# Folding a linear attention into its output projection, in hand-set order, and a new opening for the token mixer

## The chip, the cores and the metric

The kernel runs on one core of one Trainium2 chip. The metric is the device time of one execution in microseconds (us). Times are medians over several executions; the profile and trace of one execution give the rest. The span in a profile is 1.7 to 2.2 us shorter than the measured time of that execution. Some executions list a granted clock of 0.996 or 0.997 in place of 0.999 or 1.0.

## The reference

A block with two halves: a linear attention with 32 heads of 32, and a two-layer MLP over the tokens (the "token mixer"). S = 2048 tokens, D = 1024, F = 3584, bf16 inputs. The code is shortened.

```python
def _A_ref(x, wqkv, wo):
    qkv = (x @ wqkv).reshape(B, S, 3, H, Dh).transpose(2, 0, 3, 1, 4)
    q, k, v = qkv[0], qkv[1], qkv[2]
    phi = lambda t: jnp.where(t > 0, t + 1, jnp.exp(t)) + 1e-6
    pq, pk = phi(q), phi(k)
    kv = jnp.einsum("bhsd,bhse->bhde", pk, v)
    z = jnp.einsum("bhsd->bhd", pk)
    num = jnp.einsum("bhqd,bhde->bhqe", pq, kv)
    den = jnp.einsum("bhqd,bhd->bhq", pq, z)[..., None] + 1e-6
    return (num / den).transpose(0, 2, 1, 3).reshape(B, S, D) @ wo

def _B_ref(x, w1, b1, w2, b2):
    h = _layernorm(x, axis=-1)
    u = _gelu(jnp.einsum("bsd,sf->bdf", h, w1) + b1)
    return (jnp.einsum("bdf,fs->bds", u, w2) + b2).transpose(0, 2, 1)

h  = x + _A_ref(_layernorm(x), A_wqkv, A_wo)
h2 = h + _B_ref(_layernorm(h), B_w1, B_b1, B_w2, B_b2)
```

## The kernel before

The core has five engines. TensorE (PE) multiplies into PSUM; VectorE (DVE) and ScalarE (ACT) read PSUM and prepare operands; SyncE (SP) issues nearly all DMAs. A scheduler may move instructions within an engine's stream, unless the kernel holds them in program order with `pin`. Four stages follow one another: the projections with the sum of kv over the tokens; the attention (query projections, numerator and denominator, output projection, normalization of h); mixer 1 (h with w1); mixer 2.

In the attention each of the 16 tiles of 128 tokens gets its own numerators and denominators, its division on VectorE, and a transpose by DMA back into `pqT`; then the output projection.

```python
def attn_num_den(i):
    for j in range(ND):                       # 8 matmuls of 132 columns
        b, sl = divmod(j, JPB)
        nc.tensor.matmul(nd_ps[:, b, sl * NCOL:(sl + 1) * NCOL],
                         lhsT=pqT[:, j, i * P:(i + 1) * P], rhs=ndrhs[:, j, :], start=True, stop=True)
    # ... Ln and Exp of the denominators on ScalarE, o_sb = num * rd on VectorE
    return o_sb

def attn_transpose(i, o_sb):
    nc.sync.dma_start_transpose(out=pqT[:, :, i * P:(i + 1) * P], in_=o_sb[:])

def out_proj(i):
    xr = xrs.pop(i)
    h_bf = a3w.tile([P, D], BF16, name="h_bf")            # pool a3w: 3 buffers
    for dc in range(NDC):                                 # 2 halves of 512 columns
        ap_ = acc_tile()
        nc.scalar.copy(ap_[:, 0:CW], xr[:, dc * CW:(dc + 1) * CW])   # the residual as a seed
        # ... 8 matmuls of pqT with wo_sb added to it (cuts are marked with ...)
        nc.scalar.copy(h_bf[:, dc * CW:(dc + 1) * CW], ap_[:, 0:CW])
        nc.vector.bn_stats(st[:, dc, :], ap_[:, 0:CW])
    # ... bn_aggr, Ln, Exp
    nc.sync.dma_start(h_dram[i][:], h_bf[:])

def normalize_h(i):
    dst = hE if i % 2 == 0 else hO                        # even tiles, odd tiles
    nc.vector.tensor_scalar(dst[:, i // 2, :], h_bfs.pop(i)[:], ...)
    if i % 2 == 1:
        combine(hE[:, q, :], hO[:, q, :], hT2[:, q, :], hT3[:, q, :], hT4[:, q, :])   # 4 VectorE ops
```

The mixer uses the seven products of the Strassen-Winograd scheme, M1 to M7, for each pair of output tiles. From the second group of pairs on, M1 and M5 are themselves split into seven half-sized "inner" products, whose matmuls (`psI`, 256 columns) alternate with those of an outer product, in the hope that PE has outer work while VectorE and ScalarE add up the inner ones:

```python
def interleave(self, n, fs):
    # ... steps of the outer products fs, cut into four parts
    for f in (n.i1, 0, n.i6, n.i2, 1, n.i5, n.i7, 2, n.i3, 3, n.i4):
        fill(f) if isinstance(f, int) else f()

def run_pair(st, pend, nxt, ...):             # the first two pairs of mixer 1, one after the other
    st.p1()
    # ...
    if not pend:
        h = st.nk // 2
        st.p5(list(range(st.nk - 1))); st.p2(list(range(h))); st.p5([st.nk - 1])
    # ... p6, rest of p2, p7, p3, with the weight sums for the next pair between them
```

## Time and profile before

| | before |
|---|---|
| time, median of 3 | 573.17 us (573.12 to 573.37) |
| span of the profiled execution | 571.5 us |
| PE busy | 563.7 us, 99% |
| last kv accumulation to first mixer matmul ("attention") | 109.64 us |
| mixer 1 | 167.53 us |
| mixer 2 | 165.03 us |
| PE waits in mixer 1, by matmul start times | 3.1 us |

The stage lengths and PE waits here and below are worked out from the start times of the matmuls in the trace: a wait is what the distance between two starts has above columns / 2400 + 0.0025 us, which is the pace at which the matmuls of this kernel follow one another (0.216 us for 512 columns, 0.109 us for 256).

The first lines of the profile page of before: busy time by engine, and the chain of waits, that is, the chain of work that ended last, as shares of the span.

```profile
span 571.5 us, 8308 instructions
...
PE 563.7 (99%) x3124; PEld 293.3 (51%) x3124; DVE 390.2 (68%) x759; ACT 272.0 (48%) x585; POOL 1.8 (0%) x8
...
PE 95%; DVE 3%; ACT 1%; issue 1%; DMA 1%; ACTq 0%
```

PE is the bound almost everywhere. VectorE at 68% is not on the chain. A gain must come from less PE work or from the few PE waits.

The timeline of PE in the attention of before (start, duration, engine, line, operation, output <- input, count; in after, L208 is the line of a helper through which all held instructions go, so there the tile names tell them apart; SPq is SyncE's queue):

```profile
134.55 0.63 PE L1118 MATMUL nd_ps<-ndrhs,pqT 128*128 128x132 bf16 x8
135.02 3.61 PE L1019 MATMUL acc_t<-xnT,wq_sb 128*128 128x512 bf16 x16
```

Each tile's numerator and denominator take 0.47 us (from 134.55 to 135.02), 7.5 us for the 16 tiles. The printed durations have PE's latency in them; starts are what to subtract.

The timeline of PE where mixer 1 opens, in before; in brackets, the idle time before a group and what ended it:

```profile
235.50 1.68 PE L297 MATMUL psA<-hE,wq 128*128 128x512 f16 x7
237.34 0.38 PE L297 MATMUL psA<-hE,wq 128*128 128x512 f16 x1 [0.15 <-DVE hE L1189]
...
239.96 1.02 PE L297 MATMUL psA<-hO,wq 128*128 128x512 f16 x4 [0.74 <-ACT psB L316]
```

M1 (psA) runs out of normalized tiles, and M2 waits for the ScalarE copy that frees psA. With two smaller waits these are 1.46 us by start times.

### The profile page before, as it was taken

What the parts mean: (1) busy time and instruction counts of PE and PEld (TensorE: products, weight loads), DVE (VectorE), ACT (ScalarE), POOL (GpSimd) and SP (SyncE); (2) the same over time, 40 slices, a digit from 0 to 9 for tenths busy, and PEclk for the clock granted to TensorE, in tenths of its full rate; (3) what the DMA queues carried; (4) which work ended last, traced back from release to release, by engine and by line L of the source; (5) the groups of instructions that cost most, each with busy time, mean ns of one, the idle gap of its engine ahead of it and who ended that gap; (6) DMA issues with size and microseconds to landing.
All of it is one profiled execution on the core that took longest, in us unless ns stands there. A gap on an engine that the chain in (4) does not pass through costs nothing.

```text
span 571.5 us, 8308 instructions
## 1 busy us (share of the span) xinstructions
PE 563.7 (99%) x3124; PEld 293.3 (51%) x3124; DVE 390.2 (68%) x759; ACT 272.0 (48%) x585; POOL 1.8 (0%) x8
## 2 busy tenths in 40 slices
PE   7999999999999999999999999999999999999997
PEld 3444444455554444346555565555445655645643
DVE  6898887546767879873735627453979749659625
ACT  4747777666667776445445354453220411311211
POOL 1000000000000000000000000000000000000000
PEclk9999999999999999999999999999999999999999
DMA  9933432029536753104041340413892932912111
GB/s 303 357 76 79 89 74 38 19 96 323 118 72 127 177 178 111 55 2 147 1 148 28 120 148 1 148 48 81 205 255 84 244 96 75 278 56 73 38 47 46
DMA packets 97800, 66.61 MB, mean 117 GB/s; under 512 B 32082, under 2 KB 91744, under 8 KB 97760
## 3 DMA queue, kind: packets, MB, share of 16 engines
q1 hardware_dynamic: 97024, 65.42, 41.7%
q10 hardware_dynamic: 672, 0.66, 0.3%
q8 instruction: 24, 0.39, 0.3%
q14 instruction: 16, 0.13, 0.1%
q0 software_dynamic: 64, 0.01, 0.0%
HBM read 50.34 MB, written 8.39 MB: 103 GB/s over the span
## 4 chain that ended last, share of the span: by engine, by line
PE 95%; DVE 3%; ACT 1%; issue 1%; DMA 1%; ACTq 0%
PE psB L297 10%; PE psC L297 10%; PE acc_t L1019 9%; PE acc_t L1167 9%; PE psC L208 7%; PE psA L297 7%; PE psI L230 7%; PE psB L208 6%; PE psI L208 6%; PE psB L750 4%; PE psC L750 4%; PE psA L750 4%; PE psA L208 3%; PE acc_t L674 2%; PE psE L750 2%; PE psE L297 1%
## 5 line engine op out<-in xcount | busy, mean ns | idle before, releaser
L297 PEld LDWEIGHTS <-sa 128*128 128x128 f16 x436 | 42.6, 98 | 46.8 <-issue 0.7
L1019 PE MATMUL acc_t<-xnT,wq_sb 128*128 128x512 bf16 x256 | 58.0, 379 | 0.0
L1167 PE MATMUL acc_t<-wo_sb,pqT 128*128 128x512 bf16 x256 | 56.1, 379 | 0.0
L208 PEld LDWEIGHTS <-wq 128*128 128x128 bf16 (+1 forms) x357 | 34.5, 98 | 31.3
L297 PEld LDWEIGHTS <-wq 128*128 128x128 bf16 (+1 forms) x324 | 31.6, 98 | 33.1 <-issue 1.0
L208 PE MATMUL psC<-gs,wq 128*128 128x512 f16 (+2 forms) x210 | 45.0, 365 | 0.0
L1167 PEld LDWEIGHTS <-pqT 128*128 128x128 bf16 x256 | 24.8, 98 | 29.0
L1019 PEld LDWEIGHTS <-wq_sb 128*128 128x128 bf16 x256 | 24.5, 98 | 27.4
L166 ACT ACTIVATE e_sb<-acc_t 128x512 bf16<-128x512 f32 x40 | 23.9, 597 | 26.5 <-PE acc_t L1019 24.3
L170 DVE TENSOR_SCALAR e_sb<-e_sb 128x512 bf16<-128x512 bf16 x64 | 18.5, 289 | 25.4 <-ACT e_sb L166 24.8
L208 PEld LDWEIGHTS <-sa 128*128 128x128 f16 x231 | 22.6, 98 | 18.6
L750 PEld LDWEIGHTS <-xs 128*128 128x128 f16 x208 | 20.0, 98 | 23.3 <-DVE xs L736 1.3
L208 DVE TENSOR_TENSOR ot<-ot,hr 128x512 bf16<-128x512 bf16 (+2 forms) x27 | 11.2, 415 | 28.1 <-ACT ot L406 27.7
L333 ACT COPY psC<-psB 128x512 f32<-128x512 f32 x22 | 12.5, 570 | 35.1 <-PE psB L297 21.5
L297 PE MATMUL psB<-hT,sa 128*128 128x512 f16 x112 | 28.4, 379 | 0.0
L441 DVE TENSOR_TENSOR e<-psI,es 128x256 f32<-128x256 f32 x12 | 5.1, 425 | 34.0 <-PE psI L230 34.0
L297 PE MATMUL psC<-hT,wq 128*128 128x512 f16 x112 | 28.3, 379 | 0.0
L750 PE MATMUL psA<-wkv,xnT 128*128 128x512 bf16 x104 | 26.7, 379 | 0.0
L1178 DVE BATCH_NORM_STATS2 hst<-acc_t 128x6 f32<-128x512 f32 x32 | 22.1, 692 | 6.7 <-ACT h_bf L1177 6.5
L297 PE MATMUL psA<-hO,wq 128*128 128x512 f16 x112 | 25.6, 379 | 0.7 <-ACT psB L316 0.7
L297 PE MATMUL psB<-hO,sa 128*128 128x512 f16 x112 | 25.5, 379 | 0.0
L297 PE MATMUL psC<-hT,sa 128*128 128x512 f16 x112 | 25.5, 379 | 0.0
(184 smaller groups left out, 1022.9 us busy)
## 6 DMA issues: line engine op xcount, KB each, us to landing
wq<-in_B_w_dram SPq DMA_DIRECT2D x14, 1024.0 KB, 7.7
wq<-in_B_w_dram SPq DMA_DIRECT2D x8, 1792.0 KB, 9.1
xr<-in_A_x_dram SPq DMA_DIRECT2D x16, 256.0 KB, 3.1
h_dram<-h_bf SPq DMA_DIRECT2D x16, 256.0 KB, 2.2
hr<-h_dram SPq DMA_DIRECT2D x32, 128.0 KB, 2.4
out_dram<-ot SPq DMA_DIRECT2D x31, 128.0 KB, 1.8
x_sb<-in_A_x_dram SPq DMA_DIRECT2D x15, 256.0 KB, 3.2
wkv<-in_A_wqkv_dram SPq DMA_DIRECT2D x2, 1024.0 KB, 9.0
```

The lines of the kernel that those rows point to most:

```text
L166: pin(nc.scalar.activation(e_sb[:], src, ACT.Exp))
L170: pin(nc.vector.tensor_scalar(e_sb[:], e_sb[:], 1.0, PHI_EPS, ALU.min, ALU.add))
L208: return (lambda *a, **kw: pin(op(*a, **kw))) if Held.on else op
L230: pe.matmul(ps, lhsT=self.lhs[m][:, k, :], rhs=self.mov[m][:, k, :], start=(start and k == 0), stop=(k == self.nk - 1), skip_group_check=True,
L297: pe.matmul(ps[:, cols], lhsT=lhs[:, k, :], rhs=mv(k)[:, cols], start=(start and k == 0), stop=(k == self.nk - 1), skip_group_check=True,)
L333: nc.scalar.copy(self.C[:], self.B[:])
L441: dve.tensor_tensor(self.sts[m].e[:, self.cols(h)], ps, es, ALU.add)
L674: mm = nc.tensor.matmul(pp[:, 0:CW], lhsT=xnT[:, kt, i * P:(i + 1) * P], rhs=wkv[:, kt, c * CW:(c + 1) * CW], start=(kt == 0), stop=(kt == ...
L750: pin(nc.tensor.matmul(ps[:], lhsT=lhs[:, k, :], rhs=rhs[:, k, :], start=(start and k == 0), stop=(k == hk2 - 1), skip_group_check=True,))
L1019: nc.tensor.matmul(qp[:, 0:SW], lhsT=wq_sb[:, kt, j * P:(j + 1) * P], rhs=xnT[:, kt, u * SW:(u + 1) * SW], start=(kt == 0), stop=(kt == ND ...
L1167: nc.tensor.matmul(ap_[:, 0:CW], lhsT=pqT[:, j, i * P:(i + 1) * P], rhs=wo_sb[:, j, dc * CW:(dc + 1) * CW], start=(j == 0 and not SEED_RES ...
L1178: nc.vector.bn_stats(st[:, dc, :], ap_[:, 0:CW])
```

## The change

Three parts. **Folding:** kv is folded into wo once (8 transposes, 16 matmuls of 512 columns); denominators are made for 512 tokens at once, with four 32-column matmuls side by side on PE's columns; their reciprocals are written to DRAM and broadcast back over the partitions; VectorE scales `pqT` with them, and the output projection uses the folded weights. Nearly everything in this part is held in program order, on all engines. **Mixer 1's opening:** M1 and M2 of both first pairs come first, and the first M5 is an inner product. **Evacuations:** large evacuations of interleaved outer products are issued behind the inner copies. The diff, cut to its core:

```diff
+    hv, ht, hs, hd = (Held(e, True) for e in (nc.vector, nc.tensor, nc.scalar, nc.sync))   # always pinned
 ...
-            def attn_num_den(i): ...          # and attn_transpose, the o_sb and nd_ps tiles
+            def fold(j):
+                for c in range(NDC):
+                    cols = slice(c * CW, (c + 1) * CW)
+                    ps = acc_tile()
+                    ht.matmul(ps[:, 0:CW], lhsT=kvT[:, j, :], rhs=wo_sb[:, j, cols], start=True, stop=True)
+                    (hs.copy if c == 0 else hv.tensor_copy)(wf[:, j, cols], ps[:, 0:CW])
+
+            def den_mm(u):
+                ps = ndp.tile([P, SW], F32, tag="den", name="den_ps")
+                for o in range(2):
+                    for g in range(4):
+                        j = 4 * o + g
+                        ht.matmul(ps[g * QR:(g + 1) * QR, :],
+                            lhsT=zz[:, j, (1 - o) * HB:(1 - o) * HB + QR],
+                            rhs=pqT[:, j, u * SW:(u + 1) * SW],
+                            start=(o == 0), stop=(o == 1), ..., tile_position=(0, g * QR))
+                return ps
+
+            def den_inv(u, ps):
+                rd = a3d.tile([P, SW], FP16, tag="rd", name="rd")
+                hs.activation(ps[:], ps[:], ACT.Ln, bias=eps_den[:], scale=1.0 / S)
+                hs.activation(rd[:], ps[:], ACT.Exp, scale=-1.0)
+                hd.dma_start(rd_dram[u][:], rd[:])
+                rows = rd_dram[u].rearrange("(g o h) n -> o h g n", g=4, h=HB)
+                for h in range(2):
+                    rdb = a3d.tile([P, NH, SW], FP16, tag="rdb", bufs=3, name="rdb")
+                    for q in range(HB):
+                        hd.dma_start(rdb[q * DH:(q + 1) * DH, :, :],
+                            rows[h, q].unsqueeze(0).to_broadcast([DH, 4, SW]))
+                    rdbs[u, h] = rdb
+
+            def scale_q(u, h):
+                v = pqT[:, h * NH:(h + 1) * NH, u * SW:(u + 1) * SW]
+                hv.tensor_tensor(v, v, rdbs.pop((u, h))[:], ALU.mult)
 ...
+            scale_at = {0: (NSC - 2, 1), 4: (NSC - 1, 0), 5: (NSC - 1, 1)}
             for i in range(NS):
-                if i % 2 == 0 and i // 2 < TPC:
-                    attn(NS - TPC + i // 2)
 ...
-                out_proj(i)
-                if i >= 2:
-                    normalize_h(i - 2)
+                seed(i + 1)
+                out_mm(i)
+                if i == 0:
+                    den(NSC - 1)
+                load_xr(i + XRL + 2)
+                if i > 0:
+                    h_scale(i - 1)
+                if i == NS - 1:
+                    normalize_h(i - 2)
+                    normalize_h(i - 1)
+                out_evac(i)                        # h_bf copies, statistics, store of h
+                if i in scale_at:
+                    scale_q(*scale_at[i])
+                if 2 <= i < NS - 1:
+                    normalize_h(i - 2)
 ...                                            # and the first weight sums, spread over the tiles
-            for f in (n.i1, 0, n.i6, n.i2, 1, n.i5, n.i7, 2, n.i3, 3, n.i4):
+            for f in (n.i1, after1, 0, n.i6, n.i2, 1, n.i5, n.i7, flush, 2, n.i3, 3, n.i4, flush):
 ...
-    pend = run_pair(cur, [], nxt)
 ...
-    pend = run_pair(cur, pend, nxt, after1=sums1, after5=sums5)
+    Held.on = True
+    sums5()
+    cur.mov5 = mov5
+    pend, nxt = cur.run_first(quad1(1), sums1)     # p1 p1 p2 p2, inner M5 with both p6, p7 p7 p3 p3
```

## The prediction

> **What bounds the kernel now.** TensorE. The page gives PE 99% of the 571.5 us span, and the chain of waits is PE for 95%. The chain also shows the pace: 16 matmuls of 512 columns in 3.45 us (0.216 us each), 8 of 256 in 0.87 us (0.109 us), and every num/den block of 8 x 132 columns adds 0.47 us between q units. Summing these costs over all 3124 matmuls gives 558 us; by matmul start times only about 9 us of the span is PE waiting, more than half of it in the first 20 us, which the change leaves alone. Only less PE work, or the few waits after 130 us, can pay. The timeline shows those: 1.5 us where the mixer opens (PE waits at 237.3 for the normalized hE tile, at 240.0 for the copy psA to psB, 0.74 us), 0.8 us at 261-270, and about 0.2 us in each of five later inner/outer interleaves: near 3.3 us in all.
>
> **What the change does to PE work** (estimates from those durations):
> - removes 128 num/den matmuls: -7.4 us;
> - adds 8 kv transposes (+0.5) and 16 fold matmuls of 512 columns, kv into wo (+3.5);
> - adds 32 denominator matmuls of 512 columns in four 32-column positions. The Trainium skill, "TensorE: Matmul & The Clock Gate", Part 3, says matmuls in different column groups run concurrently (2.38x for three); "TensorEngine Tiling (Array Packing)", Key Properties, says a mode switch drains the array. No run of this kernel shows either. Concurrent: 8 x 0.216 us plus eight drains, I estimate 3 us in all; serial: 6.9 us;
> - first M5 of mixer 1 as 28 half matmuls (3.05 us) for 16 full ones (3.45): -0.4 us.
> Sum: about -0.8 us; +3 us if the column groups do not overlap.
>
> **Off the critical path.** DVE loses o_sb (23 us) and the memset, gains eight 128x2048 scalings (about 1.2 us each by similar tiles), 8 fold evacuations and earlier mixer sums. ACT loses the small Ln/Exp (8.5 us), gains eight 128x512 ones (0.6 each), a kvT copy and 8 fold copies (0.58): in the fold stretch about 1.8 us per 2.16 us of PE. DMA loses 16 transposes and gains four round trips: write (about 2.2 us), then eight 128 KB broadcasts, against a scaling placed some 10-11 us later. That is tight, as a late broadcast stops DVE and then PE; five accumulators absorb a few us.
>
> **Waits removed.** M1 and M2 of both pairs give 7 us of work while the last tile is normalized, so the 1.5 us at the opening should nearly vanish. Large evacuations behind the inner copies should remove most of the 0.2 us per interleave and part of the 0.8: together -2.5 us. New small waits at transposes, mode switches and the first scaling: +0.3 to +1 us.
>
> **Prediction.** -0.8 - 2.5 + 0.5: 570.3 us rounded in the change's favour to 570.0; range 566.5 to 573.5. Faster by over 2%: 2%; within 2%: 96%; slower by over 2%: 2%.
>
> **What would show each step.** Matmul start times in the denominator groups: about 0.22-0.3 us per group of four if concurrent, 0.86 if serial. The timeline between last output projection and inner M5: no PE wait above 0.2 us. Interleaves: psI waits under 0.05 us. PE waits after 130 us near 1 us in sum. DVE scaling not waiting for DMA over 2 us. Mixer 2 unchanged.
>
> **What would make it wrong.** Serial column groups (+3.9 us); the scaling late, starving the q units; the first weight sums held, in program order, behind a weight load queued behind the broadcasts; evacuations pushed later holding a PSUM tile that the next product needs.

## More of the kernel before

Later interleaves look like this, on PE and, in the second fence, on VectorE:

```profile
309.43 0.81 PE L297 MATMUL psC<-hT,wq 128*128 128x512 f16 x3
310.19 0.60 PE L230 MATMUL psI<-hE,is 128*128 128x256 f16 x4
```

```profile
309.70 0.43 DVE L434 TENSOR_TENSOR psA<-psI,es 128x256 f32<-128x256 f32 x1 [1.71 <-PE psI L230]
```

Three matmuls of 512 columns take 0.65 us, and 310.19 is 0.76 us after 309.43: a wait of 0.11 us. VectorE's sum, which frees a psI tile, ends at 310.13.

## The result, and the profile after

| | before | after |
|---|---|---|
| time, median | 573.27 us (4 runs, 573.12 to 573.37) | 577.65 us (4 runs, 577.13 to 578.10) |
| span of the profiled execution | 571.5 us | 575.4 us |
| PE busy | 563.7 us | 563.4 us |
| attention | 109.64 us | 112.52 us |
| mixer 1 | 167.53 us | 168.45 us |
| mixer 2 | 165.03 us | 165.03 us |

The ratio of after to before is 1.0076 (95% interval 1.0059 to 1.0094). A ratio is the mean time of one kernel's fast runs over that of the other's of the same rounds, so not quite the ratio of the medians. The change is 4.4 us slower, and the predicted range, 566.5 to 573.5 us, misses it. The page of after:

```profile
span 575.4 us, 8158 instructions
...
PE 563.4 (98%) x3064; PEld 289.3 (50%) x3064; DVE 387.5 (67%) x734; ACT 274.7 (48%) x573; POOL 1.8 (0%) x8
...
PE 85%; DVE 9%; ACT 3%; DMA 1%; issue 1%; DVEq 0%; ACTq 0%
```

PE has fallen from 95% to 85% of the chain and VectorE has risen to 9%. In the list of PE's waits three lines belong to the changed stages (engine, line, waited for: us in total, times, longest). Before's list has no line like the first; it has 0.2 us for the second and 0.7 us for the third:

```profile
PE acc_t L208 <- ACT acc_t L208: 3.2, 3, 2.3
PE psA L208 <- DVE hE L208: 1.8, 1, 1.8
...
PE psA L208 <- ACT psB L317: 0.4, 1, 0.4
```

The first is in the output projection. PE there, on the timeline of after:

```profile
182.53 13.99 PE L208 MATMUL acc_t<-wo_sb,pqT 128*128 128x512 f16 x64
198.85 7.07 PE L208 MATMUL acc_t<-wo_sb,pqT 128*128 128x512 f16 x32 [2.33 <-ACT acc_t L208]
206.47 3.61 PE L208 MATMUL acc_t<-wo_sb,pqT 128*128 128x512 f16 x16 [0.54 <-ACT acc_t L208]
210.38 5.80 PE L208 MATMUL acc_t<-wo_sb,pqT 128*128 128x512 f16 x25 [0.30 <-ACT acc_t L208]
```

By start times the waits there are 2.50, 0.71, 0.46 and 0.25 us: 3.9 us. Before had none above 0.05 us in this stretch. PE waits for ScalarE's seeds (acc_t). ScalarE itself, in the same stretch:

```profile
197.24 1.07 ACT L208 CAST h_bf<-acc_t 128x512 bf16<-128x512 f32 x2 [5.11 <-DMA h_dram<-h_bf]
198.19 1.12 ACT L208 CAST acc_t<-xr 128x512 f32<-128x512 bf16 x2
```

It stood 5.11 us in front of a copy of h because all three h_bf buffers were still waiting for their stores, and the seeds stand behind that copy. Why did the stores take so long? SyncE's queue:

```profile
184.05 0.34 SPq L208 DMA_DIRECT2D rd_dram<-rd  x1
187.53 3.65 SPq L208 DMA_DIRECT2D rdb<-rd_dram  x8
...
191.75 0.36 SPq L208 DMA_DIRECT2D h_dram<-h_bf  x1
```

The queue writes the reciprocals, waits 3.1 us until they have landed, issues eight broadcasts in 3.65 us (0.46 us each), then a load of x, and only then the first store of h, which lands at 197.14. The wait and the issues together hold the store back about 7 us. Its landing is slow as well, with the broadcasts and loads of x in flight: 5.4 us in place of 2.0, the median of this kernel's 16 stores of h. e2 shows which of the two matters.

The second place is the opening of mixer 1. PE, then VectorE:

```profile
238.33 1.67 PE L208 MATMUL psA<-hE,wq 128*128 128x512 f16 x7
241.77 2.10 PE L208 MATMUL psA<-hE,wq 128*128 128x512 f16 x9 [1.76 <-DVE hE L208]
244.26 2.97 PE L208 MATMUL psA<-hO,wq 128*128 128x512 f16 x13 [0.39 <-ACT psB L317]
```

```profile
238.88 0.54 DVE L208 TENSOR_SCALAR hO<-h_bf,mv_all,sc_all 128x1024 f16<-128x1024 bf16 x1
239.45 0.42 DVE L208 TENSOR_TENSOR hT<-hO,hE 128x512 f16<-128x512 f16 x1
...
240.83 0.42 DVE L208 TENSOR_TENSOR hT<-hO,hT 128x512 f16<-128x512 f16 x1
241.18 0.54 DVE L208 TENSOR_SCALAR hE<-h_bf,mv_all,sc_all 128x1024 f16<-128x1024 bf16 x1
```

VectorE does the four ops of `combine` for tiles 12 and 13 (239.45 to 241.18) before it normalizes tile 14, the very tile that PE waits for from 239.8 on. The two waits are 1.93 and 0.56 us, 2.5 in place of 1.46. (e2 shows that 0.7 us of this is lateness handed on by the first place.)

Two more terms of the prediction can be read in the same trace. One was right, the denominators, PE:

```profile
134.59 0.61 PE L208 MATMUL den_ps<-pqT,zz 128*32 128x512 bf16 x8
135.14 1.04 PE L208 MATMUL acc_t<-xnT,wq_sb 128*128 128x512 bf16 x4
```

Eight matmuls of 512 columns are done in 0.55 us; 3 to 4 ns lie between the starts of four of a group, 0.22 us between the groups. The other was wrong: the interleaves wait as before, not less. 313.57 is 0.83 us after 312.74, 0.19 us too many.

```profile
312.74 0.81 PE L208 MATMUL psC<-hT,wq 128*128 128x512 f16 x3
313.57 0.60 PE L208 MATMUL psI<-hE,is 128*128 128x256 f16 x4
```

The balance of the attention: 1.1 us less PE work (see e2), 3.9 us of new waits, hence 2.8 more (2.88 measured). Mixer 1, by start times: 0.4 us less work; opening waits +1.1 (those between its first and last matmul); the first interleaves (0.76 to 0.31) -0.45; the later ones (0.98 to 1.63) +0.65; hence +0.9 (0.92 measured).

### The profile page after: what moved, and what is told of

It reads as the page before. It is cut to its first block, busy times and chain, and to the rows that moved or that the text cites. A ratio compares the mean times of both kernels' runs of the same rounds, so it can differ in the third digit from the quotient of the medians.

```text
span 575.4 us, 8158 instructions
## 1 busy us (share of the span) xinstructions
PE 563.4 (98%) x3064; PEld 289.3 (50%) x3064; DVE 387.5 (67%) x734; ACT 274.7 (48%) x573; POOL 1.8 (0%) x8
## 4 chain that ended last, share of the span: by engine, by line
PE 85%; DVE 9%; ACT 3%; DMA 1%; issue 1%; DVEq 0%; ACTq 0%
PE psC L208 15%; PE psB L208 15%; PE psI L208 13%; PE acc_t L208 9%; PE psA L208 7%; PE psB L796 4%; PE psC L796 4%; PE psA L796 4%; DVE hst L208 4%; PE acc_t L720 2%; PE psA L298 2%; PE acc_t L1065 2%; PE psB L298 2%; PE psE L796 2%; PE psC L298 2%; DVE hT L208 2%
## 5 line engine op out<-in xcount | busy, mean ns | idle before, releaser
L208 PEld LDWEIGHTS <-wq 128*128 128x128 bf16 (+1 forms) x653 | 63.3, 98 | 57.3 <-issue 2.7
L208 PEld LDWEIGHTS <-sa 128*128 128x128 f16 x651 | 63.7, 98 | 54.7
L208 PE MATMUL acc_t<-wo_sb,pqT 128*128 128x512 f16 x256 | 56.3, 379 | 3.3 <-ACT acc_t L208 3.2
L208 PEld LDWEIGHTS <-is 128*128 128x128 f16 x376 | 36.7, 98 | 18.4 <-issue 3.6
L208 PE MATMUL acc_t<-xnT,wq_sb 128*128 128x512 bf16 x192 | 43.4, 379 | 0.0
L208 PEld LDWEIGHTS <-wq_sb 128*128 128x128 bf16 x192 | 18.5, 98 | 23.0 <-issue 1.3
L208 DVE TENSOR_TENSOR e<-psI,es 128x256 f32<-128x256 f32 x20 | 8.5, 424 | 31.9 <-ACT es L254 19.3
L208 DVE BATCH_NORM_STATS2 hst<-acc_t 128x6 f32<-128x512 f32 x32 | 20.7, 688 | 12.4 <-ACT h_bf L208 12.1
L208 DVE TENSOR_TENSOR psA<-psI,es 128x256 f32<-128x256 f32 x18 | 7.8, 432 | 27.0 <-PE psI L208 21.8
L241 ACT COPY psI<-psI 128x256 f32<-128x256 f32 x19 | 6.9, 361 | 38.3 <-PE psI L208 38.2
```

The costliest lines, as they stand in the source:

```text
L208: return (lambda *a, **kw: pin(op(*a, **kw))) if self.always or Held.on else op
L241: nc.scalar.copy(self.b, self.a)
```

## The experiments

Fourteen kernels ran, in five batches, with before timed beside each batch (medians 573.19 to 573.33 us). All gave correct results. The theory for the first batch: the stores of h jam behind the broadcasts (T1), and the hand-set order of VectorE and ScalarE causes the opening's waits (T2). Rivals: VectorE is overloaded by the 1.22 us scalings (A), or the broadcasts take the DMA bandwidth (B).

### e1: six h_bf buffers

```diff
-            a3w = a3.enter_context(tc.tile_pool(name="a3w", bufs=3))
+            a3w = a3.enter_context(tc.tile_pool(name="a3w", bufs=6))
```

> The changed kernel with six h_bf buffers in place of three; nothing else, same instruction order on every engine. Theory (the stores of h land late because they queue behind the broadcasts of the last denominator, and with three buffers the ScalarE copy of h waits 5.1 us for one): with six buffers no copy waits for a store, the 2.5 us PE wait at the fourth output tile is gone and so are the three after it (0.7, 0.5, 0.25 us); the entry waits of the mixer (1.9 + 0.6 us) shrink as VectorE is no longer behind. Time 4 to 6 us under the changed kernel: 572 to 574 us. Rival A (VectorE has too much work in this stage, the late scalings above all): PE waits of like size appear a few tiles later, time within 1 us of 577.6. Rival B (DMA bandwidth is short): waits move to the loads of x, time over 576.

Measured: 573.69 us (573.04 to 575.88), 4.0 less than after, attention 109.72 us. (The profiled execution was the slowest, 575.88 us. Its extra time lies in the first 20 us, where PE waits 1.9 us more than in before, and not in the attention.) One wait remains in the output stage, 1.19 us, and ScalarE's timeline tells why:

```profile
198.63 1.11 ACT L208 CAST acc_t<-xr 128x512 f32<-128x512 bf16 x2 [3.22 <-DMA xr<-in_A_x_dram]
```

A load of x stood in the same jammed queue. More buffers treat the stores only; the jam is still there.

### e2: the last broadcasts behind the second store

```diff
                 if i == 0:
-                    den(NSC - 1)
+                    den(NSC - 1, False)        # writes the reciprocals, no broadcast yet
 ...
                 out_evac(i)
+                if i == 1:
+                    den_bcast(NSC - 1)
```

> The changed kernel, three h_bf buffers, but the eight broadcasts of the last denominator are issued after the store of the second h tile, not before the first. Theory (order in the one issuing queue is the cause): store of the first h tile is issued about 6 us earlier (near 185 to 186 in place of 191.75) and lands in 2 to 3 us, the 2.5 us PE wait goes, the small ones behind the two late scalings (0.7, 0.5, 0.25 us) may stay: 3 to 5 us under the changed kernel, 573 to 575. Rival B (bandwidth: the broadcasts slow every transfer): store still lands late, PE wait of 1 us or more remains, time over 576.

Measured: 572.81 us (572.51 to 574.49), 4.8 less than after; attention 108.54 us. SyncE's queue and PE in e2:

```profile
184.01 0.34 SPq L208 DMA_DIRECT2D rd_dram<-rd  x1
184.41 0.42 SPq L208 DMA_DIRECT2D xr<-in_A_x_dram  x1
184.98 0.34 SPq L208 DMA_DIRECT2D h_dram<-h_bf  x1
...
188.29 4.12 SPq L208 DMA_DIRECT2D rdb<-rd_dram  x8
```

```profile
182.50 51.97 PE L208 MATMUL acc_t<-wo_sb,pqT 128*128 128x512 f16 x240
234.31 1.67 PE L208 MATMUL psA<-hE,wq 128*128 128x512 f16 x7
```

The store leaves at 184.98 instead of 191.75 and 240 matmuls run without a break. The same scalings on VectorE and the same bytes in the DMAs cause no wait: A and B fall, T1 stands. B's slow landings are real, as the two stores of h behind the broadcasts here take 4.9 and 5.3 us to land, but issued in this order they hold nobody up. The attention is now 1.10 us shorter than before's 109.64, the folding's PE saving. The first wait at the opening has shrunk too, from 1.93 to 1.20 us, with the order there unchanged: 0.7 us of it was VectorE's lateness from the jam.

### e3: the last normalizations moved

```diff
                 if i == NS - 1:
-                    normalize_h(i - 2)
                     normalize_h(i - 1)
                 out_evac(i)
+                if i == NS - 1:
+                    normalize_h(i - 2)
```

> The changed kernel with only the last VectorE work of the output stage reordered: the even tile 14 is normalized ahead of tile 13 and its four combinations, and the statistics of tile 15 come before tile 13. Theory (the order at the entry itself makes PE wait there): the 1.9 us wait within the first product is gone, the wait before the second product is between 0.3 and 0.8 us, time about 1.8 us under the changed kernel, 575.5 to 576.3. Rival (the entry waits are only inherited lateness of VectorE from the jam of the stores): VectorE is still behind at this point, so PE waits by the same sum elsewhere at the entry, time within 0.7 us of 577.6.

Measured: 576.46 us (576.19 to 577.85), 1.2 less than after, though the intervals of the two ratios overlap (1.0044 to 1.0070, and 1.0059 to 1.0094). In the trace the first opening wait (1.93 us) is gone, but PE now waits four times a little, 1.75 us in all in place of 2.5, first for ScalarE's copy, then for VectorE, which has the postponed work to do:

```profile
242.65 3.76 PE L208 MATMUL psA<-hO,wq 128*128 128x512 f16 x16 [0.36 <-ACT psB L317]
...
248.20 0.61 PE L208 MATMUL psI<-hi,is 128*128 128x256 f16 x4 [0.28 <-DVE hi L208]
```

T2 is half right: the order matters, but this order only moves most of the wait.

### e4: evacuations at once again

```diff
-                        f(ks, late)
+                        f(ks)
```

> The changed kernel with the third part of the change undone: the large copies and activations of the interleaved outer products are issued at once again, not behind the inner copies. My prediction valued this part at about 1 us. Theory now (the short PE waits in the interleaves are for the VectorE sums of the inner products, which the part does not touch): interleave waits stay at 0.1 us each, time within 0.6 us of 577.6. The prediction's view: 1 us or more slower, 578.5 or over.

Measured: 578.31 us (576.93 to 579.46), against 577.65 of after: no more than the scatter between repeats of one folded kernel. It misses both expected ranges by a little, above 578.2 and below 578.5. Two of its five runs list the lower clock; the other three took 576.93, 577.73 and 578.31 us, against 577.13 and 577.61 of after at the full clock. The built instruction lists of the two kernels explain it: the order on ScalarE, PE and SyncE is the same with and without this part (on VectorE three pairs of neighbours change places). The scheduler had already put the evacuations behind the inner copies. The third part of the change is a no-op.

### e5: e1 and e2 together, and the normalization one tile earlier

Six buffers, late broadcasts, and for the last tiles `normalize_h(i - 1)` in place of `i - 2`.

> The changed kernel with the later broadcasts (as e2), six h_bf buffers, and normalization one tile behind instead of two from tile 11 on, so that tile 14 is normalized before the statistics of tile 15 without four combinations ahead of it. Theory (two separate causes, stores queued behind broadcasts and the VectorE order at the entry): no PE wait in the output stage, entry waits in sum under 0.9 us in place of 1.8 in e2, time 0.8 to 1.6 us under e2 of the same kind of run: 571.2 to 572.0, under the kernel before by 1.3 to 2.1 us. Rival (VectorE is simply full in the last tiles, any order waits): entry waits of 1.5 us or more in sum, time within 0.5 us of e2's 572.8.

Measured: 572.16 us (571.73 to 572.39), ratio 0.9980 (0.9966 to 0.9994). The opening still waits 0.34 + 0.56 us, the sum just expected; the time misses the expected range by 0.2 us.

### e6: the mixer parts alone, on the old attention

Before with the new `run_first`, `interleave`, `run`; the first weight sums and those of the inner M5 are spread over output tiles 3 to 11; the attention is untouched.

> The kernel before with only the mixer part of the change (the opening with both pairs' M1 and M2, first M5 inner, evacuations behind inner copies, held order in mixer 1), attention left as it was. My prediction valued this part at -0.4 us of PE work and -2.5 us of waits: 570.5. Theory now (the opening does not remove the waits, it only moves them to other operands, and the interleave waits are not ScalarE's): 0 to 1 us under the kernel before, 572.3 to 573.4.

Measured: 570.82 us (570.64 to 570.90), ratio 0.9956 (0.9943 to 0.9968). PE runs through the opening:

```profile
235.34 3.62 PE L209 MATMUL psA<-hE,wq 128*128 128x512 f16 x16
238.79 3.40 PE L209 MATMUL psA<-hO,wq 128*128 128x512 f16 x15
```

Here the expectation was wrong, and the first prediction's part for the mixer right: I had come to think that the new opening waits by itself. It does so only behind the hand-set attention.

### e7 and e8: the hand-set order let go for the output stage

```diff
             xctx.close()
+            for held in (hv, ht, hs, hd):
+                held.always = False
```

e7 is after with this; e8 is e2 with it.

> The changed kernel with the hand-set order lifted in the output stage only (its instructions no longer held, the scheduler orders them; q stage and mixer as in the change). The scheduler puts the first store of h ahead of the broadcasts and splits the statistics of a tile by halves among other VectorE work. Theory (the stall and the entry waits both come from the hand-set order of the output stage, not from folding or from the opening): no PE wait over 0.3 us from 182 to the end of the first products, time 569.5 to 571.5, under the mixer part alone (570.8) by up to 1 us as folding saves about 0.9 us of PE work. Rival (folding itself loads VectorE and the queue too much): PE waits of over 1.5 us in sum remain there, time over 572.

> As e7, and the last broadcasts after the second store as in e2. Theory: within 0.6 us of e7, as the scheduler has already put the first store ahead; if e7 still shows a stall at the third to fifth output tile, this one removes it: 569.5 to 571.5.

Measured: e7 574.76 us (574.44 to 575.06), e8 572.85 us (572.29 to 573.82). Both miss 569.5 to 571.5 and lie in the rival's range (over 572), e7 with PE waits of 3.0 us in sum, and e8 is 1.9 us under e7 where 0.6 at most was expected. The scheduler makes other choices, not better ones: it scatters a denominator group between output matmuls (0.65 us of wait), and in e7 it still puts the broadcasts ahead of the second store and places two scalings back to back on VectorE ahead of a tile's statistics, which holds up ScalarE and, for 1.25 us, PE. VectorE, then PE, of e7:

```profile
200.41 2.35 DVE L1219 TENSOR_TENSOR pqT<-pqT,rdb 128x2048 bf16<-128x2048 bf16 x2
```

```profile
204.05 1.24 PE L1253 MATMUL acc_t<-wo_sb,pqT 128*128 128x512 f16 x5 [1.09 <-ACT acc_t L1248]
```

So letting go of the order does not mend it. By these two runs alone the rival, that folding itself is too much for VectorE and the queue, could stand; e9, which holds another order, decides.

### e9: e5 with the combinations behind the last normalizations

```diff
+            def combine_h(q):
+                combine(hE[:, q, :], hO[:, q, :], hT2[:, q, :], hT3[:, q, :], hT4[:, q, :], hv)
 ...
-                    normalize_h(i - 1)
+                    normalize_h(i - 1, i < NS - 2)      # tile 13 without its combination
 ...
             h_scale(NS - 1)
+            combine_h(NSP - 2)
             normalize_h(NS - 1)
```

> As e5, and the four combinations of tiles 12 and 13 are put behind the statistics of tile 15. Theory (what remains of the entry waits in e5, 0.3 us for the even tile 14 and 0.6 us for the copies behind the last Ln and Exp, is VectorE order alone): both under 0.15 us, 0.5 to 1.0 us under e5, 571.0 to 571.8; level with the mixer part alone (570.8) or a little better, as folding saves 0.9 us of PE work. Rival (VectorE is short of time, not badly ordered): waits of the same sum move to the inner M5, whose sums come later, time within 0.3 us of e5's 572.2.

Measured: 570.60 us (570.51 to 571.61), ratio 0.9959 (0.9947 to 0.9971). The opening has no wait at all:

```profile
234.75 3.62 PE L208 MATMUL psA<-hE,wq 128*128 128x512 f16 x16
238.20 3.62 PE L208 MATMUL psA<-hO,wq 128*128 128x512 f16 x16
```

This settles T2, and against the rival of e7: with the same folded attention neither the output stage nor the opening waits. So holding an order is not the fault; this order was. It also beats both kernels. But it is no faster than e6, although its attention is 0.93 us shorter (108.54 against 109.47).

### e10 and e11: the folding alone, with the old mixer

e10 has the attention part of the change and the old opening; e11 is e10 with e2's edit.

> The kernel before with only the folded attention of the change in its hand-set order; mixer 1 opens as before. Theory (the jam of the stores costs about 4 us, entry behind a late VectorE 1 to 2.5 us more, folding saves 0.9): 576.5 to 579. With the mixer part alone at -2.5 us the two parts then add up to more than the whole, or to about the whole (+4.4) if they do not act on each other: +6.9, 580. Rival (the jam comes from the mixer's earlier sums): under 575.

> As e10 with the later broadcasts of e2. Theory (without the jam folding is worth its PE work, and the entry is late by 0 to 1.5 us): 3.5 to 5 us under e10; 572.3 to 574 in itself. The prediction's view of folding: 572.8 or less.

Measured: e10 580.35 us (579.38 to 581.07), e11 575.23 us (574.68 to 577.68). The parts add up: mixer alone -2.5, attention alone +7.2, together +4.4. The jam costs 5.1 us here; 1.7 us of that in e10's trace is a stretch at half clock behind the gap (see the end), which after's trace does not have. But with the jam mended, the folding alone is still 2.0 us slower than before, though it has less PE work. The trace of e11 shows where. Up to and in the opening PE waits 2.3 us in place of 1.5, and the interleaves of mixer 1 wait 2.93 us in sum, in place of 0.98 in before. What they wait for is VectorE, which is late, and VectorE is late because a load of mixer 1's weights (wq) landed late. SyncE's issue of the second such load in before, and the VectorE op that waits for it; then the same two in e11:

```profile
288.11 1.00 SPq L140 DMA_DIRECT2D wq<-in_B_w_dram  x2
```

```profile
296.49 0.43 DVE L222 TENSOR_TENSOR is<-wq 128x512 f16<-128x512 bf16 x1 [2.22 <-DMA wq<-in_B_w_dram]
```

```profile
288.05 0.99 SPq L140 DMA_DIRECT2D wq<-in_B_w_dram  x2
```

```profile
297.78 0.43 DVE L223 TENSOR_TENSOR is<-wq 128x512 f16<-128x512 bf16 x1 [3.57 <-DMA wq<-in_B_w_dram]
```

Issued at the same place, the load is usable after 9.73 us in place of 8.38. It is the same load: 2080 packets, 2.1 MB.

### e12, e13, e14: the phase of the instruction fetches

The trace has the DMA records by queue, and the profile calls queue 8's "instruction": 24 records of 16 KB in a run, one per about 127 matmuls in every kernel. One matmul comes with one weight load, so one record per about 254 PE instructions. The Trainium skill, "Runtime: NRT & Kernel Launch", section "Instruction fetch mechanics", says that an engine's instructions are refilled in 16 KiB blocks of 256 instructions, over a DMA queue that its sequencer drives, and that the cost is "mostly hidden". Size and count agree with this trace. Whether it is hidden is the question. For each pair of weight loads of mixer 1, its length in us (first packet to the end of the last), and in brackets when a record of queue 8 began, counted from the first packet, if inside the load or less than 0.5 us ahead of it:

```
            load 1       load 2       load 3       load 4        load 5
before      6.65         6.77         6.69         6.82 (6.33)   6.57 (6.40)
e6          6.75         6.93 (6.79)  6.66 (6.51)  6.73 (6.69)   6.70 (6.30)
e11         6.68 (6.68)  8.13 (5.33)  8.01 (5.25)  6.98 (-0.40)  7.19
after       8.00 (5.19)  7.77 (0.11)  7.14 (-0.37) 6.94          6.98
e9          7.91 (5.15)  7.67 (-0.05) 7.10 (-0.34) 6.79          7.12
```

A load with such a record inside takes 7.8 to 8.1 us, one with it just ahead 7.0 to 7.7, one with it near its end 6.6 to 6.9 in these kernels. The other eight traces of e1 to e10 fit: each load in which a record began 0.0 to 5.4 us after the first packet took 7.6 to 8.2 us. (Load 5 of the folded kernels has a shorter record of the other instruction queue, 14, inside.) The folding has 60 PE instruction pairs less than before, so its fetches fall elsewhere. If this is the cause (theory P), it has nothing to do with what the folding computes, and any kernel can be made slower or faster by shifting its PE instruction count. Three kernels shift it and change nothing else: query projection units of 512 columns are done in two halves of 256, at the same PE time within 0.1 us.

```diff
+                parts = 2 if 8 <= u * ND + j < 8 + N else 1    # N: 6 in e12, 3 in e13, 2 in e14
+                w = SW // parts
-                for kt in range(ND):
-                    matmul(qp[:, 0:SW], ..., rhs=xnT[:, kt, u * SW:(u + 1) * SW], ...)
+                for c in range(parts):
+                    for kt in range(ND):
+                        matmul(qp[:, c * w:(c + 1) * w], ..., rhs=xnT[:, kt, u * SW + c * w:u * SW + (c + 1) * w], ...)
```

The built lists of VectorE, ScalarE and SyncE are identical with those of the kernels they come from, instruction by instruction.

> The kernel of e9 with six of its q projection units (units 8 to 13) computed in two halves of 256 columns: 48 more matmuls, each half as long, so 0.1 us more PE work by the 216 and 109 ns that the traces show; everything else unchanged. Theory P (phase of the instruction fetches): in e9's trace the records of DMA queue 8 (kind instruction, 16 KB each, about 1.1 us) come once per 127 matmuls, and a load of mixer 1's weights with such a record inside it takes 7.7 to 8.0 us in place of 6.4 to 6.9; 48 more matmuls ahead of mixer 1 move the records about 9 us earlier, out of the first three loads. P expects: those loads 6.4 to 7.0 us, VectorE's waits for them below 2.5 us in sum (4.3 in e9), mixer 1 165.2 to 165.6 us (165.97 in e9), time 570.0 to 570.3 us (570.6 in e9). Rival Q (something in the folded attention itself, such as where its buffers lie, slows the loads): loads, mixer 1 and time stay as in e9, 570.6 to 570.9 us.

> The kernel of before with three q projection units (8 to 10) in two halves: 24 more matmuls, under 0.1 us more PE work, nothing of the change in it. P: the queue-8 records, which before has at +12, +9.5, +7.6, +6.3 and +6.4 us from the start of the five loads of mixer 1, move about 4.4 us earlier, into four of the loads; these take 7.5 to 8.1 us, the inner/outer interleaves wait 2 to 3 us in sum (0.98 in before, 2.93 in e11), mixer 1 takes 168.5 to 169.6 us (167.53), time 574.2 to 575.3 us. Q: mixer 1 stays within 0.2 us of before, time 573.2 to 573.5 us.

> The kernel of e6 (the mixer part alone, no folding) with two q projection units (8 and 9) in two halves: 16 more matmuls, under 0.1 us more PE work. P: the queue-8 records, at +8.3, +6.8, +6.5, +6.7 and +6.3 us in e6, move about 3 us earlier, into four or five of the loads; the loads take 7.5 to 8.1 us, interleaves wait 1.4 to 2.0 us in sum after the first (0.98 in e6), mixer 1 165.7 to 166.3 us (165.29), time 571.3 to 571.9 us (570.82 in e6): the gap between the mixer part alone and the folded kernels is this phase. Q: mixer 1 stays at 165.2 to 165.4, time 570.8 to 571.0 us.

| | median, us | of | mixer 1, us | of |
|---|---|---|---|---|
| e12 (e9, 48 more matmuls) | 570.69 (570.55 to 572.34) | 570.60 | 165.80 | 165.97 |
| e13 (before, 24 more) | 574.49 (574.22 to 574.68) | 573.23 | 168.63 | 167.53 |
| e14 (e6, 16 more) | 571.78 (571.33 to 573.66) | 570.82 | 166.27 | 165.29 |

```
            load 1       load 2       load 3       load 4        load 5
e12         6.77         6.75         6.90         6.71          7.25 (6.73)
e13         6.65         6.73 (6.33)  6.85 (6.62)  6.78 (6.59)   7.91 (6.52)
e14         6.71 (6.71)  6.86 (6.86)  6.92 (6.59)  7.84 (6.45)   8.22 (4.68)
```

The sixth load, of mixer 2's weights, is 8.20 us in e13 and 7.77 in e14 in place of 6.4. The records did not move as evenly as the count: where they came to lie near a load's end they stopped at +6.3 to +6.9 us. There they are harmless to some loads and not to others (load 5 of e13, load 4 of e14). The packets tell why: of the 2080 in load 5 of e13, 2077 are done by +6.73 us, and the last three start at +7.67, just as the record (6.52, 1.15 us long) ends; load 4 of e14 has the same (2077 by +6.71, the last three from +7.59). It matters whether a load's last packets stand ahead of the record or behind it. So fewer loads were slowed than I expected, two in e13 and three in e14. But the times are as P said and not as Q: two kernels without any folding became 1.3 and 1.0 us slower with 24 and 16 more matmuls that take no more PE time. From 280 us on their interleaves wait 2.1 and 2.0 us, against 0.98 in both originals. The fifth load of e13, whose issue stands next to the VectorE op that waits for it, in two views of e13:

```profile
358.64 0.99 SPq L140 DMA_DIRECT2D wq<-in_B_w_dram  x2
```

```profile
368.47 0.42 DVE L222 TENSOR_TENSOR is<-wq 128x512 f16<-128x512 bf16 x1 [3.67 <-DMA wq<-in_B_w_dram]
```

That is 9.83 us; in before the same load took 8.16 (358.82 to 366.98).

e12 confirms P for the loads: all of the first four are fast, and VectorE's waits for them fall from 4.3 to 1.8 us. For the time it misses: 570.69 us is not below e9's 570.60. Its interleaves still wait 1.35 us from 280 us on (1.51 in e9, 0.98 in e6), nearly all of the excess in one wait of 0.46 us at 378. Mixer 1 misses its range too (165.80 in place of 165.2 to 165.6). In e9's trace VectorE's sum there begins 0.5 us after ScalarE's copy that it needs, in e6's 0.13 us, with no late load near; after, e1 to e5 and e9 have the same wait at the same place, e7 and e8, with another order, have not. And e9's profiled run, on which P's sum rests, was 0.5 us slower than its median. What that 0.46 us is, I did not settle. The traces give a lead: in all eight kernels it is the same VectorE op, it starts 0.4 us after the semaphore instruction ahead of it has ended (0.05 in e6), and a record of queue 14, the other instruction queue, begins 0.7 us after its start, while e6 to e8 have none within 10 us. That points to the instruction fetch of another engine, VectorE's perhaps; no run tests it.

## Why the prediction was wrong, point by point

1. **PE bound, -0.8 us of PE work: right.** The attention's PE work fell by 1.1 us where nothing jammed (109.64 to 108.54 in e2), and the inner M5 by the predicted 0.4. The term for the denominators was 3.0 us; it measured 2.6, four times 0.645: 0.55 us from a group's first start to the next other matmul, in which 0.095 us for the switch back is contained, and 0.095 us on the way in. The Trainium skill, "TensorE: Matmul & The Clock Gate", Part 3, on matmuls in different column groups, was a good guide to this.
2. **"A late broadcast stops DVE and then PE; five accumulators absorb a few us": this is the step that failed.** I asked when the broadcast's consumer needs it, and not what stands behind the broadcasts in the queue that issues them. The scaling was in time enough. The stores of h and loads of x behind eight issues and one landing were not, with three buffers to bridge. The Trainium skill, "DMA: Bandwidth & Descriptors", section "Anatomy of one DMA" (of the GpSimd path), says that "any semaphore wait happens on the issuing sequencer before dispatch"; this trace agrees (3.1 us without an issue on SyncE), and I could have drawn the conclusion from it: everything behind waits too. It cost 3.9 us of PE waits in the output stage and 0.7 us at the opening; moving the broadcasts behind the second store took them away (e2).
3. **Opening waits of 1.5 us "nearly vanish": right for the part itself, wrong for the combination.** On the old attention they vanish (e6: no wait, 570.82 us, where the terms -0.4 and -2.5 give 570.3). In after they grew to 2.5 us: 0.7 is lateness from the jam, and 1.8 stays without it (e2), because the hand-set VectorE order put four combinations ahead of the normalization that PE needs. e9 shows the same attention without the wait.
4. **"Large evacuations behind the inner copies should remove most of the 0.2 us per interleave": wrong.** That part is a no-op, as the scheduler already had that order (e4). The remaining waits of 0.1 us are for VectorE's sums. In e6, the mixer part alone, PE waits 1.9 us less than in before, in place of the 2.5 predicted: the opening's 1.46 and 0.46 of the first interleaves; the later ones wait 0.98 us as before.
5. **New small waits of +0.3 to +1 us:** mode switches measured 0.76 us (8 times 0.095, inside the 2.6 us above). None of the four named risks cost anything: the column groups overlap, no scaling waited for its broadcast, one weight sum waited 1.1 us for a load (at 170.46) but not PE for it, and the evacuations were not moved at all.
6. **Not in the prediction at all:** mixer 1's loads share the DMA engines with PE's instruction fetches, so that a change in instruction count far ahead moved mixer 1 by 1.1 and 1.0 us (e13, e14). Up to 2 us of e11's loss goes with loads delayed this way; that e13 and e14 reproduce the effect without any folding is shown, that it is the whole of e11's 2 us is argued.

In sum: -1.1 and -0.4 of work, +3.9 jam, +1.1 opening, +0.2 interleaves: +3.7 us from the terms, +3.9 in span, +4.4 in medians. Set against the predicted terms: the jam is 3.9 us that were not in the sum, the opening came out 2.5 worse (-1.5 predicted, +1.0 or +1.1 measured), the interleaves 1.2 worse (-1.0 and +0.2), PE work and small new waits together 1.2 better. Mended, the folding equals the mixer part alone: 570.6 and 570.8 us, both 2.5 us better than before. Of the folding's 0.9 us shorter attention, mixer 1 gives 0.5 to 0.7 back; the late loads are one part, one wait of 0.46 us is open.

## What to carry to other kernels

When a change puts a DMA that must wait (write to DRAM, read back) into a queue held in program order, list what stands behind it in that queue and count the buffers that bridge it; the DMA's own consumer may be the least of the worries. Try each part of a compound change alone: here one part gave all of the gain, one was a no-op and one hid two faults of order. And before explaining a difference of 1 us in a stage that the change didn't touch, look where instruction fetches fall among its loads: splitting a few matmuls at no PE cost shows whether it is that.

## What the Trainium skill lacked or had wrong

- "Runtime: NRT & Kernel Launch", "Instruction fetch mechanics": the fetch of a 16 KB block is called mostly hidden. PE doesn't wait for it here, but a 2.1 MB pair of weight loads that has one inside took 7.7 to 8.2 us in place of 6.6 to 6.9, and that cost 1.0 and 1.3 us of kernel time (e14, e13).
- "DMA: Bandwidth & Descriptors", "Anatomy of one DMA": it says where a wait happens, but draws no conclusion for the DMAs behind it. Here one landing of 3.1 us and eight broadcast issues of 0.46 us each held a store back about 7 us and cost 3.9 us.
- "TensorE: Matmul & The Clock Gate", Part 3: 2.38x is given as measured for three column groups, no measured figure for four. Here four matmuls of 32 columns start 3 to 4 ns apart, and the next four 0.22 us later, where four in a row take 0.86 us.
- "TensorEngine Tiling (Array Packing)", "Key Properties": a mode switch drains the array, without a figure. Here a start into or out of a denominator group came 0.095 us later than the pace; that this is the drain is not shown.
- "TensorE: Matmul & The Clock Gate", "Back-to-back issue gap": 131 ns is given as the sustained distance of 512-column matmuls. Here streams of them, each with its weight load, run at 216 ns, the figure that this section gives for a single one and that the page's Parts 1 and 2 give for back-to-back ones.
- The same page, Part 1: half clock after an idle window of about 3.4 us. In e10, eight matmuls after a gap of 2.7 us between starts were 0.427 us apart, and the trace's granted clock is half for 3.41 us from 199.0; after the same gap in the trace of after, all ran at 0.216 us. So a shorter gap can do it, in some runs.
